# Loading the key weight in two halves, normalising tiles 0 and 3 in halves, and a new order of the whole program

## The chip, the core and the metric

The kernel runs on one core of one Trainium2 chip. The metric is the device time of one execution in microseconds (us), as the median of three runs. A core has five engines that run side by side, each with its own queue that it works through in order: PE (TensorE, the matrix products; the trace lists its weight loads apart as PEld), DVE (VectorE), ACT (ScalarE), POOL (GpSimd) and SP (SyncE, which here only issues DMA transfers). An engine waits at an instruction until what it reads is written, and everything behind it in its queue waits too. The products go to PSUM, which has eight banks; a bank can be written again only when the reader of its last contents is done.

## The reference, cut to what matters

```python
x = A_x                                   # 1 x 2048 x 512, bf16
h = x + _A_ref(_layernorm(x), A_wqkv, A_wo)
h2 = h + _B_ref(_layernorm(h), B_w1, B_w2)

def _A_ref(x, wqkv, wo):                  # linear attention, 32 heads of 16
    q, k, v = split(x @ wqkv)
    phi = lambda t: jnp.where(t > 0, t + 1, jnp.exp(t)) + 1e-6
    pq, pk = phi(q), phi(k)
    kv = jnp.einsum("bhsd,bhse->bhde", pk, v)
    z = jnp.einsum("bhsd->bhd", pk)
    num = jnp.einsum("bhqd,bhde->bhqe", pq, kv)
    den = jnp.einsum("bhqd,bhd->bhq", pq, z)[..., None] + 1e-6
    return (num / den) @ wo

def _B_ref(x, w1, w2):                    # 512 -> 1792 -> 512
    return jnp.maximum(x @ w1, 0) @ w2
```

## The kernel before

The 2048 rows of x are cut into 16 tiles of 128 rows, and four tiles make a chunk. The whole program is one list of words, ORDER. A loop reads it from left to right and calls one small function for each word, and each function puts its instructions at the end of the queues of its engines. So the order of the words is the order of each engine's queue; nothing else schedules. The last lines of the kernel are that loop:

```python
    for word in ORDER.split():
        name, *idx = word.split(".")
        ops[name](*map(int, idx))
```

The words, in the order of the work (t is a tile, c a chunk, b a PSUM bank):

- `lx.t.n` loads n tiles of x, `lk.k.n`, `lq`, `lv`, `lo`, `l1`, `l2` load n of the K-slices of the weights of keys, queries, values, output and of the two dense layers. All are DMA transfers that SP issues.
- `warm.n.b.w` runs n products on zeros, before there is data.
- `S.t` and `A.t` (DVE) take mean and variance of a row; `R.t.n` (ACT, two activations) makes 1/sqrt(var + eps) for n tiles; `N.t` (DVE, line 268) writes the normalised tile to `h_nat`. `N.t.k.n` does so for n column blocks of 128 from block k on.
- For the tiles 0 to 4, `T.t.b` (PE, line 293, four products with the identity) transposes the normalised tile into bank b and `E.t` (ACT, line 303) copies it to `lnT`. `T.t.b.k.n` and `E.t.k.n` do n of the four blocks. The other tiles are transposed by a DMA, `X.t` (line 314).
- `K.t.b` (PE, line 322) is the key product of a tile, four matmuls over the four K-slices; `K.t.b.k.n` does n of them. `F`, `U` (ACT) and `M`, `D` (DVE) make phi of it. `Q.c.j.b`, `qF`, `qU`, `qM`, `qD` do the same for the queries.
- `G.t` (PE, line 374) sums key times normalised x over the tiles; `za`, `zf`, `zhi`, `zlo` (DVE) sum the keys themselves, and `z.j.b` (PE, line 398) finishes z. `kv`, `m`, `d4`, `dl4`, `dx4`, `wb`, `rb`, `ab`, `dm` make the product with values and output weight, and the denominator, which goes through DRAM and comes back spread over the partitions (`rb`, `ab`).
- `h.t.b` (PE, line 502) and `hD.t` (DVE) give h; `s`, `a`, `r`, `n` normalise it, and `x.t` (SP, line 315) transposes it by DMA into `lnT` of its chunk.
- `p.c.f.b` and, in halves of the columns, `ph` (PE, lines 517 and 526) are the first dense layer, `pD.c.f.2` (DVE, line 537) its relu for two of the 14 slices; `f.t.b.f0.n` (PE, line 546) is the second layer, `fo.t` (DVE, line 554) adds h, and `fd.t` writes the result.

The key product takes its pieces by two arguments:

```python
    def op_K(t, b, k=0, n=KD):
        ...
        for kd in range(k, k + n):
            nc.tensor.matmul(
                bk[:, b, :], lhsT=lnT[c][:, kd, j * P : (j + 1) * P], rhs=wk_sb[:, kd, :],
                **part(("k", t), KD),
            )
```

Of the kernel before, what the change touches and what calls it, by code (L numbers as in the profile page):

```python
# [23 lines left out]
R.8.2 G.0 S.15 F.4.2 N.8 G.1 S.13 X.8 U.4.2 S.14 G.3 qU.0.2.2 A.13 S.12 lv.0.2 G.2 M.4.2 A.12 N.9 K.7.3 R.12.2
A.15 D.4.2 X.9 qF.0.2.2 K.6.2 N.12 A.14 S.11 R.14.2 X.12 K.8.0 F.6.2 N.15 N.14 G.4 A.11 N.13 U.6.2 M.6.2 X.13
qM.0.0.2 K.9.1 R.10.2 qD.0.0.2 K.12.2 X.15 D.6.2 U.8.2 za.4.1 G.5 F.8.2 X.14 K.13.3 N.11 N.10 za.6.0 G.6 X.11
U.12.2 G.7 M.8.2 F.12.2 X.10 qM.0.2.2 K.14.0 D.8.2 M.12.2 K.15.1 lv.2.2 za.8.0 l1.0.2 K.11.3 l1.2.2 F.14.2 D.12.2
K.10.2 zf U.14.2 qD.0.2.2 G.9 zhi F.10.2 M.14.2 G.13 zlo U.10.2 G.8 M.10.2 D.14.2 G.12 D.10.2 z.0.0 z.2.0 z.3.0
# [568 lines left out]
```

## Time and profile before

| | |
|---|---|
| time, median of 3 runs | 169.2 us (169.2 to 169.52) |
| the profiled execution's own time | 169.35 us |
| its span, first to last instruction | 167.6 us |
| PE busy, instructions | 162.9 us, 97%, 920 products |
| DVE busy | 115.9 us, 69% |
| ACT busy | 49.5 us, 30% |
| mean granted TensorE clock | 0.999 |
| DMA | 16.28 MB, mean 97 GB/s |

The profile's page gives the busy time of each engine and its share of the span. Between the span and the time of the execution lie 1.75 us that the profile does not show. The chain of waits follows the execution back from its last instruction; each of its rows has a start, a length, and the instructions with their line. A timeline row has the start, the busy time, the engine, the line, the operation, what it writes and reads, and in brackets how long the engine had been idle and who ended that. A row of the windows view has, for one stretch, the length and then the busy time of each engine with its number of instructions.

### The profile page before, as it was taken

How to read it: one execution, taken by the hardware profiler on the slowest of the kernel's cores; microseconds unless marked ns; L12 is line 12 of the kernel's file. 1: busy time of each engine (PE TensorE's matmuls, PEld its weight loads, DVE VectorE, ACT ScalarE, POOL GpSimd, SP SyncE). 2: the span in 40 equal slices, each digit the busy share in tenths (PEclk: the TensorE clock that was granted, in tenths of full speed). 3: DMA queues.
4: the chain of work that ended last, by engine and by line, in shares of the span. 5: the costliest groups of instructions: out<-in, count | busy, mean ns of one | idle time of the engine just before them, and what ended most of it. 6: DMA issues, size and time to landing. Idle time of an engine off the chain costs nothing.

```text
span 167.6 us, 2414 instructions
## 1 busy us (share of the span) xinstructions
PE 162.9 (97%) x920; PEld 79.8 (48%) x920; DVE 115.9 (69%) x215; ACT 49.5 (30%) x83; POOL 4.8 (3%) x21
## 2 busy tenths in 40 slices
PE   7899999999999999999999999999999999999992
PEld 7444444454544674444444444444444444564441
DVE  3899999952499979668999899564535484400632
ACT  3799997625687925300000020010000000000000
POOL 7400000000000000000000000000000000000000
PEclk9999999999999999999999999999999999999999
DMA  4974464773651546140353034312000000020131
GB/s 108 353 294 118 107 121 94 246 288 94 153 195 36 124 126 218 60 133 29 101 98 88 0 61 89 104 30 64 0 0 4 31 0 0 21 83 2 47 104 60
DMA packets 26091, 16.28 MB, mean 97 GB/s; under 512 B 16096, under 2 KB 25056, under 8 KB 26080
## 3 DMA queue, kind: packets, MB, share of 16 engines
q1 hardware_dynamic: 25760, 15.87, 33.5%
q10 hardware_dynamic: 320, 0.26, 0.6%
q8 instruction: 7, 0.11, 0.3%
q14 instruction: 4, 0.03, 0.1%
HBM read 9.96 MB, written 2.62 MB: 75 GB/s over the span
## 4 chain that ended last, share of the span: by engine, by line
PE 93%; DVE 2%; DMA 1%; ACT 1%; issue 0%
PE bk L546 28%; PE bk L517 26%; PE bk L374 8%; PE bk L322 8%; PE bk L330 8%; PE bk L502 8%; PE bk L526 3%; DMA x_nat<-in_A_x_dram 1%; DVE st L254 1%; PE bk L446 1%; DVE gT L554 1%; PE bk L398 1%; DVE h_nat L268 1%; PE bk L420 1%; PE bk L432 1%; PE bk L293 1%
## 5 line engine op out<-in xcount | busy, mean ns | idle before, releaser
L546 PE MATMUL bk<-w_sb,at 128*128 128x512 bf16 (+2 forms) x252 | 50.9, 355 | 0.0
L517 PE MATMUL bk<-lnT,w_sb 128*128 128x512 bf16 x200 | 45.6, 379 | 0.0
L537 DVE TENSOR_SCALAR at<-bk 128x1024 bf16<-128x1024 f32 x27 | 32.4, 1221 | 13.6 <-PE bk L517 10.6
L546 PEld LDWEIGHTS <-at 128*128 128x128 bf16 x252 | 23.5, 98 | 25.2 <-DVE at L537 0.3
L517 PEld LDWEIGHTS <-w_sb 128*128 128x128 bf16 x200 | 19.5, 98 | 23.1 <-issue 0.4
L554 DVE SCALAR_TENSOR_TENSOR gT<-bk,rstd,h_nat 128x512 bf16<-128x512 f32 (+2 forms) x18 | 12.1, 688 | 22.6 <-PE bk L546 20.2
L340 ACT ACTIVATE eb<-bk 128x1024 bf16<-128x1024 f32 (+1 forms) x18 | 16.6, 930 | 3.5 <-PE bk L420 1.6
L260 ACT ACTIVATE rstd<-mv,eps 128x2 f32<-128x2 f32 (+2 forms) x14 | 4.1, 295 | 45.1 <-DVE mv L257 41.6
L343 ACT ACTIVATE rb<-bk 128x1024 bf16<-128x1024 f32 (+1 forms) x18 | 16.6, 935 | 0.9 <-PE bk L322 0.9
L502 PE MATMUL bk<-m_sb,pqs 128*128 128x512 bf16 x64 | 15.3, 379 | 0.0
L322 PE MATMUL bk<-wk_sb,lnT 128*128 128x512 bf16 x64 | 15.0, 379 | 0.0
L330 PE MATMUL bk<-lnT,wq_sb 128*128 128x512 bf16 x64 | 15.0, 379 | 0.0
L374 PE MATMUL bk<-at,h_nat 128*128 128x512 bf16 x56 | 13.2, 379 | 0.0
L254 DVE BATCH_NORM_STATS2 st<-x_nat 128x6 f32<-128x512 bf16 x16 | 10.5, 676 | 2.1 <-DMA x_nat<-in_A_x_dram 2.1
L508 DVE TENSOR_TENSOR h_nat<-bk,x_nat 128x512 bf16<-128x512 f32 x16 | 10.7, 679 | 1.1 <-PE bk L502 1.0
L256 DVE BATCH_NORM_STATS2 st<-h_nat 128x6 f32<-128x512 bf16 x16 | 10.8, 686 | 0.2
L502 PEld LDWEIGHTS <-pqs 128*128 128x128 bf16 x64 | 6.3, 98 | 7.6
L374 PEld LDWEIGHTS <-h_nat 128*128 128x128 bf16 x64 | 6.1, 97 | 7.3 <-issue 0.2
L322 PEld LDWEIGHTS <-lnT 128*128 128x128 bf16 x64 | 6.0, 98 | 7.4 <-DMA lnT<-h_nat 0.4
L330 PEld LDWEIGHTS <-wq_sb 128*128 128x128 bf16 x64 | 6.1, 98 | 7.1 <-issue 0.2
L347 DVE TENSOR_SCALAR eb<-eb 128x1024 bf16<-128x1024 bf16 (+1 forms) x18 | 6.7, 390 | 0.3 <-ACT eb L340 0.3
L268 DVE TENSOR_SCALAR h_nat<-x_nat,mv,rstd 128x512 bf16<-128x512 bf16 x16 | 6.2, 406 | 0.6 <-ACT rstd L261 0.5
(62 smaller groups left out, 90.9 us busy)
## 6 DMA issues: line engine op xcount, KB each, us to landing
w_sb<-in_B_w_dram SPq DMA_DIRECT2D x4, 896.0 KB, 5.2
out_dram<-gT SPq DMA_DIRECT2D x15, 128.0 KB, 1.9
rr<-scr SPq DMA_DIRECT2D x28, 64.0 KB, 2.6
x_nat<-in_A_x_dram SPq DMA_DIRECT2D x2, 512.0 KB, 7.0
x_nat<-in_A_x_dram SPq DMA_DIRECT2D x4, 128.0 KB, 2.7
wk_sb<-in_A_wqkv_dram SPq DMA_DIRECT2D x1, 512.0 KB, 4.1
x_nat<-in_A_x_dram SPq DMA_DIRECT2D x2, 256.0 KB, 4.4
wq_sb<-in_A_wqkv_dram SPq DMA_DIRECT2D x1, 512.0 KB, 5.8
```

The source lines that it names most:

```text
L254: op_S = lambda t: nc.vector.bn_stats(out=st[:, t, :], in_=x_nat[:, t, :])
L256: op_s = lambda t: nc.vector.bn_stats(out=st2[:, t, :], in_=h_nat[:, t, :])
L322: nc.tensor.matmul(bk[:, b, :], lhsT=lnT[c][:, kd, j * P : (j + 1) * P], rhs=wk_sb[:, kd, :], **part(("k", t), KD),)
L330: nc.tensor.matmul(bk[:, b, :], lhsT=wq_sb[:, kd, j * P : (j + 1) * P], rhs=lnT[c][:, kd, :], start=(kd == 0), stop=(kd == KD - 1),)
L340: nc.scalar.activation(out=buf(eb, kind, i, n), in_=bank(at_bank[kind, i], n), func=ACT.Exp)
L343: nc.scalar.activation(out=buf(rb, kind, i, n), in_=bank(at_bank[kind, i], n), func=ACT.Relu)
L374: nc.tensor.matmul(bk[:, KD + kd, :], lhsT=ln_nat[:, t, kd * P : (kd + 1) * P], rhs=pk(t)[:, 0, :], start=(not stated), stop=(len(stated) ...
L502: nc.tensor.matmul(bk[:, b, :], lhsT=pqs[:, (c * KD + jb) % NQ, j * P : (j + 1) * P], rhs=m_sb[:, jb, :], start=(jb == 0), stop=(jb == KD ...
L517: nc.tensor.matmul(bk[:, b, :], lhsT=w1_sb[:, kd, f * P : (f + 1) * P], rhs=lnT[c][:, kd, :], start=(kd == 0), stop=(kd == KD - 1),)
L537: nc.vector.tensor_scalar(out=acts[c % 2][:, f : f + n, :], in0=bank(at_bank["p", c, f], n), scalar1=-1.0, scalar2=0.0, op0=ALU.mult, op1= ...
L546: nc.tensor.matmul(bk[:, b, 0 : w * P], lhsT=acts[c % 2][:, f, j * P : (j + 1) * P], rhs=w2_sb[:, f, k * P : (k + w) * P], **part(("f", t, ...
L554: nc.vector.scalar_tensor_tensor(out=o_t[:, t % NO, cols], in0=bk[:, at_bank["f", t, k], 0 : w * P], scalar=rstd2[:, t : t + 1], in1=h_nat ...
```

## The change

Only the list of words changes. Its line numbers grow by one, since the new list is one line longer.

- The key weight is loaded by two transfers, `lk.0.2` and `lk.2.2`, with tile 3 of x between them, in place of one transfer ahead of tile 3. The query weight now goes ahead of the tiles 6 and 7.
- DVE takes the mean and variance of tile 2 before it normalises any tile; then it normalises tile 1, tile 0 in two halves, and tile 2. Tile 3 is normalised in two halves, with other work between.
- PE transposes tile 1 first, then tile 0 in two halves and tile 2. The first key products are of tiles 1 and 2, each in two halves; those of tile 0 and tile 3 follow, in halves too.
- From there on the list has the same words in another order and with other banks: the loads of the value and output weights, the keys, the sums, the heads, the two dense layers.

```diff
-table const lx.0.1 warm.66.7.64 lx.1.1 masks lx.2.1 lk.0.4 lx.3.1 S.0 lx.4.2 S.1 lx.6.2 lq.0.4 A.0 A.1 S.2 R.0.1
-warm.2.7 lx.8.4 R.1.1 N.0 lx.12.4 A.2 N.1 T.0.1 R.2.1 T.1.6 E.0 N.2 E.1 T.2.4 S.3 K.0.2 E.2 A.3 S.4 K.1.4.2.2
...
+table const lx.0.1 warm.66.7.64 lx.1.1 masks lx.2.1 lk.0.2 lx.3.1 S.0 lk.2.2 S.1 lx.4.2 lq.0.4 A.0 A.1 S.2
+warm.2.7 R.1.1 lx.6.2 R.0.1 lx.8.4 A.2 N.1 R.2.1 lx.12.4 N.0.2.2 T.1.0 N.0.0.2 N.2 T.0.6.0.2 T.0.2.2.2 E.1 S.3
...
```

The loads at the start of SP's queue, before (`x_nat` is x, 512 columns a tile; `wk_sb` and `wq_sb` are the weights of keys and queries, four K-slices of 512):

```order
L220 DMA x_nat<-in_A_x_dram 128x512 x3
L226 DMA wk_sb<-in_A_wqkv_dram 128x4x512
L220 DMA x_nat<-in_A_x_dram 128x512
L220 DMA x_nat<-in_A_x_dram 128x1024 x2
L226 DMA wq_sb<-in_A_wqkv_dram 128x4x512
L220 DMA x_nat<-in_A_x_dram 128x2048 x2
```

and after:

```order
L221 DMA x_nat<-in_A_x_dram 128x512 x3
L227 DMA wk_sb<-in_A_wqkv_dram 128x2x512
L221 DMA x_nat<-in_A_x_dram 128x512
L227 DMA wk_sb<-in_A_wqkv_dram 128x2x512
L221 DMA x_nat<-in_A_x_dram 128x1024
L227 DMA wq_sb<-in_A_wqkv_dram 128x4x512
L221 DMA x_nat<-in_A_x_dram 128x1024
L221 DMA x_nat<-in_A_x_dram 128x2048 x2
```

The first three tiles of x stay where they were; tile 3 moves ahead of the second half of the key weight, and the query weight ahead of the tiles 6 and 7.

The first statistics and normalisations on DVE, before (`st` and `mv` are what `S` and `A` write, `h_nat` what `N` writes):

```order
L254 BN_STATS st<-x_nat 128x6 x2
L255 BN_AGGR mv<-st 128x2 x2
L254 BN_STATS st<-x_nat 128x6
L268 TENSOR_SCALAR h_nat<-x_nat,mv,rstd 128x512
L255 BN_AGGR mv<-st 128x2
L268 TENSOR_SCALAR h_nat<-x_nat,mv,rstd 128x512 x2
L254 BN_STATS st<-x_nat 128x6
L255 BN_AGGR mv<-st 128x2
```

and after:

```order
L255 BN_STATS st<-x_nat 128x6 x2
L256 BN_AGGR mv<-st 128x2 x2
L255 BN_STATS st<-x_nat 128x6
L256 BN_AGGR mv<-st 128x2
L269 TENSOR_SCALAR h_nat<-x_nat,mv,rstd 128x512
L269 TENSOR_SCALAR h_nat<-x_nat,mv,rstd 128x256 x2
L269 TENSOR_SCALAR h_nat<-x_nat,mv,rstd 128x512
L255 BN_STATS st<-x_nat 128x6
L256 BN_AGGR mv<-st 128x2
```

The statistics of tile 2 (the third `BN_STATS` and the `BN_AGGR` behind it) now stand ahead of all normalisations; the first of these is tile 1's, and tile 0's are the two of 256 columns.

The DMA transposes of chunk 3 (`lnT_88`) in SP's queue, with the last one of chunk 2 (`lnT_87`) and the writes of results around them, before:

```order
L315 DMA_TRANSPOSE lnT_87<-hn 128x4x128 x4
L561 DMA out_dram<-gT 128x512
L315 DMA_TRANSPOSE lnT_88<-hn 128x4x128
L561 DMA out_dram<-gT 128x512 x2
L315 DMA_TRANSPOSE lnT_88<-hn 128x4x128 x2
L561 DMA out_dram<-gT 128x512
L315 DMA_TRANSPOSE lnT_88<-hn 128x4x128
```

and after:

```order
L316 DMA_TRANSPOSE lnT_87<-hn 128x4x128 x2
L562 DMA out_dram<-gT 128x512
L316 DMA_TRANSPOSE lnT_87<-hn 128x4x128 x2
L316 DMA_TRANSPOSE lnT_88<-hn 128x4x128 x3
L562 DMA out_dram<-gT 128x512
L316 DMA_TRANSPOSE lnT_88<-hn 128x4x128
```

Before, the last transpose of chunk 2 and the four of chunk 3 had writes between them; after, `x.11`, `x.8`, `x.12`, `x.14` and `x.15` follow each other, then one write and `x.13`. In PE's order three products of chunk 2 (`p.2.6`, `p.2.7`, `p.2.2`) now stand ahead of the first of chunk 3, `p.3.4`; before, eleven of the fourteen stood ahead of `p.3.2`.

More of the change, by code (lines that the diff above doesn't have):

```diff
@@ L24 @@
[L24 to L28, printed above, removed]
@@ new lines @@
+z.3.1 G.9 zc zh d4.0.0 G.10 dl4.0 dx4.0 G.15 wb.0 G.14 Q.1.0.2 gA.2.2 gD.0.2 rb.0.0 Q.1.1.3 ab.0.1 rb.0.6 ab.0.5
+kv.2.7 rb.0.4 kv.0.7 ab.0.7 kv.3.7 rb.0.2 kv.1.7 qF.1.0.2 Q.1.2.0 l2.7.7 kx ab.0.3 Q.1.3.1 qM.1.0.2 qU.1.0.2 m.3.7
+m.0.4 m.1.5 qU.1.2.2 qD.1.0.2 m.2.6 Q.2.0.2 mD.0.2 mA.2.2 Q.2.1.3 qF.1.2.2 dm.0.0.2 Q.2.3.7 dm.0.2.2 qF.2.0.2
+h.1.1 qM.1.2.2 qD.1.2.2 qU.2.0.2 h.0.4 hD.1 Q.2.2.6 s.1 d4.1.0 a.1 hD.0 nA.1 h.3.2 s.0 qF.2.2.2 x.1 h.2.1 a.0 hD.3
+nA.0 Q.3.3.3 s.3 qU.2.2.2 x.0 hD.2 Q.3.2.2 dl4.1 a.3 n.3 Q.3.1.5 s.2 qF.3.2.2 x.3 Q.3.0.4 a.2 n.2 qU.3.2.2
@@ new lines @@
+qM.3.2.2 x.2 qM.2.0.2 ph.0.11.1.0 qM.2.2.2 dx4.1 ph.0.1.7.0 qD.3.2.2 qU.3.0.2 ph.0.0.6.0 wb.1 ph.0.2.2.0 l2.0.7
+ph.0.10.0.0 qF.3.0.2 ph.0.3.3.0 ph.0.10.0.1 qM.3.0.2 rb.1.2 ph.0.0.6.1 qD.2.0.2 rb.1.7 ph.0.11.1.1 rb.1.3 p.0.5.5
+pD.0.10.2 rb.1.1 p.0.4.4 rb.1.5 qD.3.0.2 rb.1.0 p.0.7.1 rb.1.6 pA.0.4.2 qD.2.2.2 ph.0.1.7.1 d4.2.4.2 pD.0.0.2
+ph.0.2.2.1 dl4.2 rb.1.4 ph.0.3.3.1 dl4.3 p.0.6.0 pD.0.2.2 dx4.2 p.0.12.6 dx4.3 wb.2 r.0.4 p.0.13.7 dm.1.2.2
+p.0.8.4 dm.1.0.2 pD.0.12.2 p.0.9.5 rb.2.6 rb.2.4 h.7.2 rb.2.1 wb.3 h.6.7 rb.2.2 hD.7 rb.2.0 pD.0.6.2 h.4.6 rb.2.3
@@ new lines @@
+rb.2.7 f.0.3.0.7 rb.2.5 pD.0.8.2 hD.4 f.0.3.7.7 s.7 a.7 hD.6 h.5.6 s.4 f.3.1.7.7 n.7 dm.2.2.2 s.6 f.3.1.0.7
+dm.2.0.2 hD.5 rb.3.2 h.10.2 rb.3.5 a.4 s.5 rb.3.7 fo.3 h.8.6 rb.3.4 rb.3.1 a.5 hD.10 h.11.7 rb.3.6 a.6 n.5 rb.3.0
+n.4 f.2.1.0.7 n.6 rb.3.3 s.10 x.5 hD.8 f.2.1.7.7 hD.11 x.7 fo.0 s.8 h.9.5 fd.3 dm.3.2.2 x.6 f.1.0.0.7 dm.3.0.2
+fo.2 x.4 hD.9 h.12.4 s.9 h.15.6 a.10 h.13.3 h.14.5 hD.13 hD.12 f.1.0.7.7 hD.15 hD.14 p.1.6.2 s.12 s.11 p.1.12.4
+s.15 p.1.5.7 s.13 p.1.7.3 a.11 fo.1 n.11 p.1.10.5 pD.1.6.2 p.1.11.6 a.12 a.13 a.8 s.14 p.1.9.1 a.9 a.15 n.10 r.8.4
@@ new lines @@
+p.1.8.0 pD.1.10.2 x.10 p.1.3.3 pD.1.8.2 p.1.13.5 a.14 n.12 r.12.4 p.1.1.1 n.14 n.9 r.4.4 pD.1.12.2 x.9 p.1.0.0
+p.1.2.2 pD.1.0.2 fd.0 x.11 p.1.4.6 n.13 pD.1.2.2 f.6.4.7.7 pD.1.4.2 f.6.4.0.7 n.15 n.8 x.8 f.5.7.0.7 x.12
+f.7.0.0.7 x.14 f.4.5.0.7 x.15 f.4.5.7.7 fd.2 x.13 p.2.6.2 fd.1 p.2.7.3 p.2.2.1 pD.2.6.2 p.3.4.6 fo.4 p.2.3.2
+f.7.0.7.7 pD.2.2.2 fo.6 f.5.7.7.7 fo.7 fd.6 fd.7 p.2.12.4 fo.5 p.2.13.5 p.3.3.2 pD.2.12.2 p.3.2.1 p.2.10.0
+pD.3.2.2 p.3.8.4 p.2.11.1 p.2.4.3 pD.2.10.2 p.3.5.7 p.3.0.1 pD.3.4.2 p.3.9.5 p.3.7.6 pD.3.8.2 p.3.1.2 p.2.5.4
@@ L54 @@
+pD.3.0.2 p.3.6.5 pD.2.4.2 p.2.0.2 pD.3.6.2 p.2.9.7 p.2.1.3 p.3.13.5 p.3.12.4 p.2.8.6 p.3.10.0 pD.2.8.2 p.3.11.1
+f.13.7.0.7 pD.3.10.2 pD.2.0.2 f.10.6.7.7 pD.3.12.2 f.8.1.7.7 f.8.1.0.7 f.15.3.0.14.0.2 f.15.5.0.14.3.1 f.10.6.0.7
+fo.15.3.1 fd.15.3.1 fd.4 f.14.2.7.7 fo.8 f.14.2.0.7 fo.10 fd.8 fd.5 fo.15.0.2 f.13.7.7.7 fd.10 fd.15.0.2
+f.11.1.0.7 f.11.1.7.7 f.9.6.7.7 fo.11 fo.13 f.9.6.0.7 fd.13 fd.11 f.12.0.0.7 fo.9 fo.14 fd.9 f.12.0.7.7 fd.14
+f.15.5.0.14.2.1 fo.12 fo.15.2.1 fd.12 fd.15.2.1
 """
```

37 lines of the change are left out of this document (9 added, 28 removed).

## The prediction

> **What bounds the kernel now.** I read the page first, then the windows, then the chain of waits, and last the timeline of the first microseconds. The page has PE at 97%; the windows tell where the other 3% lie.
>
> ```profile
> 6.02:7.12 1.10, 1.04 (x8) 0.74 (x8) 0.80 (x4) 0.94 (x3) 0.16 (x1) 1.00 1.05 375
> ...
> 8.30:40.00 31.70, 31.70 (x191) 14.66 (x190) 27.19 (x69) 24.36 (x42) 0.00 (x0) 1.00 0.58 169
> 40.00:104.00 64.00, 64.00 (x340) 31.33 (x339) 55.41 (x99) 20.30 (x29) 0.00 (x0) 1.00 0.39 104
> 104.00:163.70 59.70, 59.70 (x298) 28.26 (x298) 27.26 (x30) 0.50 (x2) 0.00 (x0) 1.00 0.13 37
> ```
>
> From 8.30 to 163.70 PE is busy in every microsecond; what it lacks of 100% lies ahead and behind. So the end comes from three things alone: when PE gets its first real products, whether it ever waits after that, and the 3.9 us from 163.70 to the end of the span. The chain of waits says the same and gives the pace.
>
> ```profile
> 7.12 0.40 PE bk L293 x4
> 7.52 1.80 PE bk L322 x8
> 9.32 0.24 PE bk L293 x4
> 9.57 1.73 PE bk L322 x8
> ...
> 94.46 8.63 PE bk L517 x40
> ...
> 163.71 0.77 DVE gT L554
> ```
>
> Forty products of 512 columns take 8.63, so one takes 0.216 and four (one word `K`, `Q`, `h` or `p`) 0.863. The first eight key products take 1.80 where the next eight take 1.73: here PE waits about 0.08, on bank 4, which `E.2` must empty before `K.1` may write it. What set the start is in the timeline:
>
> ```profile
> 3.04 1.29 DVE L254 BATCH_NORM_STATS2 st<-x_nat 128x6 f32<-128x512 bf16 x2 [1.80 <-DMA x_nat<-in_A_x_dram]
> 4.24 0.30 DVE L255 BATCH_NORM_AGGREGATE mv<-st 128x2 f32<-128x6 f32 x2
> 4.84 0.69 DVE L254 BATCH_NORM_STATS2 st<-x_nat 128x6 f32<-128x512 bf16 x1 [0.30 <-DMA x_nat<-in_A_x_dram]
> 5.46 0.52 DVE L268 TENSOR_SCALAR h_nat<-x_nat,mv,rstd 128x512 bf16<-128x512 bf16 x1
> 5.89 0.16 DVE L255 BATCH_NORM_AGGREGATE mv<-st 128x2 f32<-128x6 f32 x1
> 5.98 0.38 DVE L268 TENSOR_SCALAR h_nat<-x_nat,mv,rstd 128x512 bf16<-128x512 bf16 x1
> 6.66 0.41 DVE L268 TENSOR_SCALAR h_nat<-x_nat,mv,rstd 128x512 bf16<-128x512 bf16 x1 [0.30 <-ACT rstd L261]
> ...
> 6.03 1.49 PE L293 MATMUL bk<-ident,h_nat 128*128 128x128 bf16 x12 [0.43 <-DVE h_nat L268]
> ...
> 6.67 1.09 ACT L303 ACTIVATE lnT<-bk 128x512 bf16<-128x512 bf16 x2
> ...
> 7.36 0.59 PE L322 MATMUL bk<-wk_sb,lnT 128*128 128x512 bf16 x2
> ```
>
> `S.2` waits for tile 2 of x until 4.84 and ends at 5.53; `N.0` ends at 5.98, `T.0` starts at 6.03, `E.0` at 6.67, and the first key product at 7.36, behind `T.2`, which waited for `N.2`.
>
> **The change part by part.** *The loads.* The weight is not what is waited for:
>
> ```profile
> wk_sb<-in_A_wqkv_dram SPq DMA_DIRECT2D x1, 512.0 KB, 4.1
> ...
> wq_sb<-in_A_wqkv_dram SPq DMA_DIRECT2D x1, 512.0 KB, 5.8
> ...
> 2.18 0.43 SPq L226 DMA_DIRECT2D wk_sb<-in_A_wqkv_dram  x1
> ...
> 4.16 0.43 SPq L226 DMA_DIRECT2D wq_sb<-in_A_wqkv_dram  x1
> ```
>
> Issued at 2.18 it lands at 6.3, 1.1 before the first key product. In two halves one more issue of 0.43 goes through SP, which waits for nothing there; the second half ends behind tile 3's 128 KB, a quarter of the 512 KB more, and is used two products (0.43) after the first. Gain nothing, cost nothing: the cover is those 1.1 us, and half a microsecond of lateness would cost nothing either. The tiles 0 to 2 of x are issued as before, so `S.2` keeps its 4.84 to 5.53. The query weight moves ahead of tiles 6 and 7, so these land where it does now, at 4.16 plus 5.8, 10.0. Their statistics stand on DVE behind `D.1`, and ahead of that lie the first key product (to 8.3), its exp, its relu, and a sum, some half a microsecond each, so nothing waits long for them.
>
> *The new chain to the first key product.* `A` ends 0.21 behind the last `S` (4.33 to 4.54), so `A.2` ends at 5.74; `N.1` behind an `A` took until 6.36, 0.31 after 6.05, so now until 6.05; its transposes start 0.05 later, 6.10; `E` followed `T` by 0.64, so `E.1` starts at 6.74 and, at 0.60, ends at 7.34; the key product followed the end of `E.0` (7.27) by 0.09, so `K.1` starts at 7.43. `N.2` no longer waits for its `rstd`, and `T.2` is through at about 7.2: no longer last. Before, `K.0` started at 7.36 and PE lost 0.08 behind it, in effect 7.44. Now nothing is lost there, since `K.2` finds its copy ready at 8.2, before its turn at 8.29. **The start is worth 0.01, that is nothing**: `T.2` was relieved, and `E.1` is late in its place.
>
> *The halves on DVE.* No row has 256 columns; the nearest are
>
> ```profile
> L347 DVE TENSOR_SCALAR eb<-eb 128x1024 bf16<-128x1024 bf16 x14 | 5.6, 420 | 0.3 <-ACT eb L340 0.3
> L347 DVE TENSOR_SCALAR eb<-eb 128x512 bf16<-128x512 bf16 x4 | 1.1, 284 | 0.0
> ```
>
> Twice 284 is 148 ns more than 420, so an instruction's fixed part is at most 0.15 and the two added ones cost 0 to 0.30. I take 0.2, since back-to-back instructions overlap (5.89 plus 0.16, and the next starts at 5.98). The Trainium skill (VectorE: DVE Perf Modes, section on the TRN2 errata) says that every SBUF operation pays a fixed latency and that tiles should keep at least 512 elements, which speaks against these halves; it measures the fixed part as about 150 cycles of 0.96 GHz, an estimate of 0.31 for two. The rows agree with it, and by it the sum would take the upper end.
>
> Does PE see the 0.2? DVE is full in two stretches:
>
> ```profile
> 20.00:35.00 15.00, 15.00 (x71) 6.75 (x70) 14.94 (x32) 11.91 (x17) 0.00 (x0) 1.00 0.67 180
> 86.00:106.00 20.00, 20.00 (x95) 9.02 (x93) 18.93 (x36) 0.90 (x4) 0.00 (x0) 1.00 0.31 67
> ```
>
> ```profile
> 8.70 0.41 DVE L268 TENSOR_SCALAR h_nat<-x_nat,mv,rstd 128x512 bf16<-128x512 bf16 x1 [0.24 <-ACT rstd L261]
> ...
> 34.05 1.29 DVE L350 TENSOR_TENSOR at<-rb,eb 128x1024 bf16<-128x1024 bf16 x2
> ...
> 35.56 0.19 PE L398 MATMUL bk<-ones,zhl 128*128 128x1 bf16 x2
> ```
>
> In the first it hands over the last keys at 35.34 and the z products start at 35.56, a slack of 0.2; besides, DVE stood idle 0.24 for `R.3` ahead of `N.3`, where the new order has `S.5`. Nothing, then, with that idle time as its cover; the slack of 0.2 stays.
>
> *The rest of the order.* PE has the same products, so its work is the same. What can cost is a place where it arrives early. I went through the new queues with the durations above. Two places have nothing to spare. `K.4` comes one query product behind `T.4`: PE's way is 0.24 plus 0.86, and the way over the copy 0.40 (row 7.12) plus 0.60 plus 0.09, both about 1.1. And `K.3` is due 12 products and four transposes behind 7.43, at 10.26, and needs the first half of `E.3`.
>
> ```profile
> 9.60 0.60 ACT L303 ACTIVATE lnT<-bk 128x512 bf16<-128x512 bf16 x1
> ```
>
> `E.3` ended at 10.20; now half of `E.0` stands ahead of it and half of itself behind, so its first half ends at 10.2 again, and with 0.09 to PE that is 10.29. Each place may cost 0 to 0.1; I take 0.1 for both. A copy, a transpose or a relu that comes earlier than needed costs nothing, and the other handovers keep some tenths by the same counting. The end of the list is the same: one `fo`, one quarter `fo`, two writes.
>
> The sum: 169.35 − 0.01 + 0 + 0.1 = 169.45 for the profiled execution, which stands 0.15 over the median; against the median **169.3 us**.
>
> **The rivals.** *DVE is late at z* (slower). If a half costs as much as a whole, 0.41 (row at 6.66), DVE has 0.8 more to do ahead of the z products, less the 0.2 of slack: 0.6 later, 169.9. It decides from 0.2 on. For it: DVE is at 14.94 of 15 there. Against it: the 0.24 of idle time recovered, and the L347 rows. Chance 0.14.
>
> *`x.13` is late* (slower). Chunk 3 starts earlier on PE:
>
> ```profile
> 91.00 2.59 PE bk L517 x12
> ...
> 96.59 0.85 DVE L276 TENSOR_SCALAR hn<-h_nat,mv 128x512 bf16<-128x512 bf16 x3
> ...
> 99.82 2.35 DVE L537 TENSOR_SCALAR at<-bk 128x1024 bf16<-128x1024 f32 x2
> ...
> 20.29 9.22 SPq L314 DMA_TRANSPOSE lnT<-h_nat  x7
> ...
> 97.46 4.95 SPq L315 DMA_TRANSPOSE lnT<-hn  x3
> ...
> DMA to landing us min/median/max: 2.4/2.5/4.3
> ```
>
> Chunk 1's products start at 91.00 plus one `h` word, 91.86; the fourteen end at 103.9, six `f` words of seven products at 113.0, three products of chunk 2 at 115.6: there `p.3.4` is due. DVE gets its first four products at 95.3 and has seven relus of 1.14 (2.35 for two, with an overlap), 8.0, and seven `n` of 0.26 and 1.1 of statistics, 2.9, ahead of the end of `n.8`: 106.2. Then `x.8`, `x.12`, `x.14`, `x.15` at 1.3 (9.22 for seven), a write's issue of 0.4 (as the weight's), and `x.13`, which lands 2.5 later: 114.3. It has 1.3 to spare. But three in a row took 4.95 once, 1.0 more than at 1.3 each, and one landed after 4.3: with one of these PE waits 0 to 0.6, with both 1.6. I price it at 0.6: 169.9. Chance 0.08.
>
> *Other handovers are missed*: the 0.1 to 0.4 of slack is worked out from one execution, over many places. Missing by 0.4 more in one gives 169.7. Chance 0.16.
>
> *Tile 2 of x lands early* (faster).
>
> ```profile
> x_nat<-in_A_x_dram SPq DMA_DIRECT2D x4, 128.0 KB, 2.7
> ```
>
> Tile 2 is issued just ahead of the weight's 2.18, so at 1.7, and lands at 4.8; by the median of its kind, 2.7, it would land at 4.4. Then `S.2` would start behind `A.1` at 4.5, and all that follows be 0.3 to 0.4 earlier: 168.85. For it: a smaller transfer stands behind it. Against it: nothing ahead of it changes. Chance 0.16.
>
> *The first transposes run fast* (no measurable change). Eight took 1.04 from 6.02 on, so four 0.5, and four take 0.24 at 9.32: PE is slow until about 7. At the fast pace `E.1` and with it `K.1` start some 0.2 earlier, and `T.2`, through at 7.2, allows it: 169.1. Before, this would have gained nothing, since `T.2` waited for `N.2`. The Trainium skill (TensorE: Matmul & The Clock Gate, part 1) has the clock released at the end of a free-running window of activity, so at another time in another execution; no row here shows it move. Chance 0.10.
>
> **How the numbers follow.** What a measurement here can tell from no change is about 0.2%, 0.34 us: 168.86 to 169.54. The forecast, 169.3, has 0.36, and with the fast transposes the same verdict has 0.46; their own range is 169.0 to 169.5. Late at z 0.14, `x.13` 0.08 and other handovers 0.16 make slower 0.38. Faster is the early tile, 0.16. The range takes in the early tile with the fast transposes, 168.85 − 0.2, and the slower rivals, 169.9, with the upper end of the halves, 0.1 more: 168.65 to 170.0; outside lie two of the late handovers together, and a start earlier still, less than 0.2.
>
> **What would show it.** Right: `K.1` first, at 7.4 to 7.5, PE full from there to about 163.8, and the key products without the 1.80. Wrong: a PE wait after 7.5. In the chain of waits it would stand as DVE between `G` and z near 35, as a DMA of `lnT` near 115, or as ACT `lnT` near 10 or 14. A first key product before 7.1 would make the start worth more than I say.

## The result and the profile after

The changed kernel takes 170.13 us in the median of ten runs (168.87 to 170.45), the kernel before 169.2 in ten runs beside them (168.79 to 169.55): 1.005 times as long, with a 95% interval of 1.0035 to 1.0066. I had forecast 169.3, no measurable change, and a range up to 170.0. The profiled execution took 169.87, its span is 168.2.

The windows of the changed kernel, in the columns known from before:

```profile
5.66:6.96 1.30, 1.27 (x12) 0.94 (x13) 1.30 (x4) 0.85 (x3) 0.42 (x2) 1.00 0.65 165
6.96:16.00 9.04, 8.63 (x46) 3.67 (x45) 7.69 (x24) 8.23 (x21) 0.00 (x0) 1.00 0.68 237
16.00:40.00 24.00, 24.00 (x150) 11.08 (x149) 20.32 (x49) 17.45 (x26) 0.00 (x0) 1.00 0.65 174
40.00:104.00 64.00, 64.00 (x341) 31.38 (x339) 53.99 (x98) 20.78 (x31) 0.00 (x0) 1.00 0.38 93
104.00:164.20 60.20, 60.20 (x301) 28.50 (x299) 27.51 (x31) 0.00 (x0) 0.00 (x0) 1.00 0.16 43
```

From 16.00 on PE is full, as before. Nearly all that was lost lies in the first 16 us. The timeline of PE there:

```profile
5.67 1.40 PE L294 MATMUL bk<-ident,h_nat 128*128 128x128 bf16 x12
6.96 0.60 PE L323 MATMUL bk<-wk_sb,lnT 128*128 128x512 bf16 x2
7.72 1.45 PE L323 MATMUL bk<-wk_sb,lnT 128*128 128x512 bf16 x6 [0.16 <-DMA wk_sb<-in_A_wqkv_dram]
9.39 0.29 PE L294 MATMUL bk<-ident,h_nat 128*128 128x128 bf16 x2 [0.21 <-DVE h_nat L269]
...
13.28 0.40 PE L294 MATMUL bk<-ident,h_nat 128*128 128x128 bf16 x4
13.52 1.03 PE L331 MATMUL bk<-lnT,wq_sb 128*128 128x512 bf16 x4
14.42 1.04 PE L323 MATMUL bk<-wk_sb,lnT 128*128 128x512 bf16 x4
```

The first key product starts at 6.96, 0.40 ahead of the 7.36 of before. Then PE waits three times: in the middle of `K.1`, for the second half of the weight, at `T.3` and at `T.4`. The brackets show less than is lost, since the end of a matmul is modelled; from start to start, less the pace of 0.216 of a product, the three cost 0.32, 0.38 and 0.20, and two handovers (`K.4`, and `K.11` at 30.9) 0.04 each: 0.98. Before, 0.08 and 0.03 were lost so. Together: −0.40 + 0.98 − 0.11 = +0.47; the last product starts 0.50 later (164.74, was 164.24). The two profiled executions lie 0.52 apart (169.87 and 169.35) and the medians 0.93, so this account covers the profiled pair and not all of the difference of the medians.

What DVE did meanwhile:

```profile
4.41 0.66 DVE L255 BATCH_NORM_STATS2 st<-x_nat 128x6 f32<-128x512 bf16 x1
...
7.19 0.18 DVE L256 BATCH_NORM_AGGREGATE mv<-st 128x2 f32<-128x6 f32 x1
8.39 0.69 DVE L255 BATCH_NORM_STATS2 st<-x_nat 128x6 f32<-128x512 bf16 x1 [1.02 <-DMA x_nat<-in_A_x_dram]
9.00 0.33 DVE L269 TENSOR_SCALAR h_nat<-x_nat,mv,rstd 128x256 bf16<-128x256 bf16 x1
...
11.23 1.29 DVE L255 BATCH_NORM_STATS2 st<-x_nat 128x6 f32<-128x512 bf16 x2 [0.19 <-DMA x_nat<-in_A_x_dram]
12.44 0.40 DVE L269 TENSOR_SCALAR h_nat<-x_nat,mv,rstd 128x512 bf16<-128x512 bf16 x1
12.75 0.17 DVE L256 BATCH_NORM_AGGREGATE mv<-st 128x2 f32<-128x6 f32 x1
12.84 0.38 DVE L269 TENSOR_SCALAR h_nat<-x_nat,mv,rstd 128x512 bf16<-128x512 bf16 x1
```

`S.2` no longer waits for tile 2. But `S.5` stands still for 1.02 until tiles 4 and 5 are there, with the first half of `N.3` behind it (9.00), and `T.3` behind that; `S.7` waits for tiles 6 and 7 until 11.23, and `N.4`, for `T.4`, comes two statistics later, at 12.84. The issue rows of the changed kernel (size of one, median time to landing) show that the loads came later:

```profile
x_nat<-in_A_x_dram SPq DMA_DIRECT2D x4, 128.0 KB, 2.3
wk_sb<-in_A_wqkv_dram SPq DMA_DIRECT2D x2, 256.0 KB, 3.8
x_nat<-in_A_x_dram SPq DMA_DIRECT2D x2, 256.0 KB, 5.6
```

The 3.8 is the middle of two unlike halves, and the 5.6 (4.4 before) that of two pairs of tiles. By the completion records of the trace, in which each transfer reports in sixteen parts, the weight's first half is complete at 5.25, 3.1 after its issue, and its second half at 7.68, 4.5 after its issue; the whole one was complete at 6.32, 4.1 after. Of the second half's sixteen parts fourteen had landed by 6.65; two came at 7.15 and 7.68, and PE waits for the last. Of the whole weight's parts the first landed at 5.79 and the last at 6.32. Tiles 4 and 5 are complete at 8.37 (before, 7.31), and tiles 6 and 7, which now stand behind the query weight as well, at 11.21 (8.46). All landing times below are read so, by the last part.

### The profile page after: what moved, and what is told of

The parts are those of the page before. It is cut to its first block, busy times and chain, and to the rows that moved or that the text cites. A ratio compares the mean times of both kernels' runs of the same rounds, so it can differ in the third digit from the quotient of the medians.

```text
span 168.2 us, 2408 instructions
## 1 busy us (share of the span) xinstructions
PE 163.4 (97%) x920; PEld 79.8 (47%) x920; DVE 114.9 (68%) x217; ACT 49.7 (30%) x85; POOL 4.7 (3%) x21
## 4 chain that ended last, share of the span: by engine, by line
PE 93%; DVE 2%; ACT 2%; DMA 1%; issue 0%
PE bk L547 29%; PE bk L518 26%; PE bk L375 8%; PE bk L503 8%; PE bk L331 8%; PE bk L323 7%; PE bk L527 3%; DMA x_nat<-in_A_x_dram 1%; DVE st L255 1%; ACT lnT L304 1%; PE bk L294 1%; PE bk L447 1%; PE bk L399 1%; PE bk L421 1%; PE bk L433 1%; DVE h_nat L269 0%
## 5 line engine op out<-in xcount | busy, mean ns | idle before, releaser
L547 PE MATMUL bk<-w_sb,at 128*128 128x512 bf16 (+2 forms) x252 | 49.7, 355 | 0.0
L518 PE MATMUL bk<-lnT,w_sb 128*128 128x512 bf16 x200 | 44.0, 379 | 0.0
L323 PE MATMUL bk<-wk_sb,lnT 128*128 128x512 bf16 x64 | 15.5, 379 | 0.2 <-DMA wk_sb<-in_A_wqkv_dram 0.2
L269 DVE TENSOR_SCALAR h_nat<-x_nat,mv,rstd 128x512 bf16<-128x512 bf16 (+1 forms) x18 | 6.7, 393 | 0.0
```

The lines of the kernel that those rows point to most:

```text
L323: nc.tensor.matmul(bk[:, b, :], lhsT=lnT[c][:, kd, j * P : (j + 1) * P], rhs=wk_sb[:, kd, :], **part(("k", t), KD),)
L518: nc.tensor.matmul(bk[:, b, :], lhsT=w1_sb[:, kd, f * P : (f + 1) * P], rhs=lnT[c][:, kd, :], start=(kd == 0), stop=(kd == KD - 1),)
L547: nc.tensor.matmul(bk[:, b, 0 : w * P], lhsT=acts[c % 2][:, f, j * P : (j + 1) * P], rhs=w2_sb[:, f, k * P : (k + w) * P], **part(("f", t, ...
```

## The experiments

Nearly all edit only words of ORDER; split_cols and late_issue add a small load function. The table gives the median, the ratio to the kernel before on the same chip with its interval, the share of time in which the transfer engines were busy from 5.50 to 7.50 (windows of that kernel's profile), and the landings there of the last of the weight, of tiles 4 and 5 and of tiles 6 and 7. The share adds up the times of all packets, so it can pass 1. Share and landings are those of one execution, the time is a median.

| kernel | us | ratio (95%) | share | weight | 4, 5 | 6, 7 |
|---|---|---|---|---|---|---|
| before | 169.2 | | 1.12 | 6.32 | 7.31 | 8.46 |
| before_again | 169.26, one run | | 1.09 | 6.71 | 7.74 | 9.07 |
| changed | 170.13 | 1.005 (1.0035 to 1.0066) | 0.71 | 7.68 | 8.37 | 11.21 |
| s5_late | 170.06 | 1.006 (1.0041 to 1.0078) | 0.78 | 7.41 | 8.12 | 11.28 |
| n4_early | 170.6 | 1.009 (1.0067 to 1.0112) | 0.75 | 7.12 | 8.40 | 11.24 |
| s5_n4 | 169.91 | 1.0069 (1.0034 to 1.0104) | 0.69 | 7.46 | 8.79 | 11.22 |
| split_before | 169.65 | 1.0037 (1.0022 to 1.0052) | 0.68 | 7.74 | 9.46 | 10.17 |
| whole | 169.25 | 1.0001 (0.9984 to 1.0018) | 0.99 | 6.57 | 7.60 | 9.93 |
| whole_x67 | 168.95 | 1.0 (0.9983 to 1.0017) | 1.06 | 6.41 | 7.43 | 8.16 |
| whole_x67_s5 | 169.72 | 1.0036 (1.0023 to 1.0049) | 1.07 | 6.19 | 7.21 | 8.68 |
| x3_first | 168.95 | 0.9996 (0.9981 to 1.0011) | 1.07 | 6.62 | 7.29 | 7.98 |
| adjacent | 169.79 | 1.0043 (1.0021 to 1.0066) | 0.95 | 5.84 | 7.10 | 8.04 |
| split_cols | 169.89 | 1.0042 (1.0026 to 1.0057) | 0.74 | 6.23 | 8.38 | 9.03 |
| split_touch | 169.78 | 1.0039 (1.0023 to 1.0056) | 0.82 | 7.67 | 8.71 | 9.38 |
| four_pieces | 169.86 | 1.004 (1.002 to 1.0061) | 0.94 | 6.11 | 8.63 | 9.28 |
| more_tiles | 169.04 | 0.9994 (0.9979 to 1.001) | 1.07 | 6.05 | 7.45 | 8.15 |
| wq_split | 168.92 | 0.999 (0.9972 to 1.0007) | 1.07 | 6.35 | 7.38 | 8.05 |
| other_queue | 170.82 | 1.0084 (1.0048 to 1.0119) | 1.01 | 7.00 | 8.01 | 8.73 |
| late_issue | 170.04 | 1.0072 (1.0049 to 1.0095) | 0.77 | 7.04 | 8.49 | 9.68 |
| split_lead | 169.22 | 1.0031 (1.0006 to 1.0055) | 0.78 | 7.75 | 8.41 | 9.53 |

### Is it the order of DVE?

Theory 1 took the three waits as a series in which the last decides. First, the statistics out of the way of `N.3`:

```diff
- R.3.1 S.5 K.2.3.0.2 ... N.3.0.2 A.5 S.4 T.3.5.0.2 ... N.3.2.2 E.3.0.2
+ R.3.1 K.2.3.0.2 ... N.3.0.2 T.3.5.0.2 ... N.3.2.2 S.5 A.5 S.4 E.3.0.2
```

> The changed kernel with one edit: S.5 A.5 S.4 stand behind both halves of N.3 on DVE, no longer ahead of them. In the changed kernel DVE stood idle 1.02 us at S.5 for the tiles 4 and 5 of x (8.37), and PE waited 0.38 us for the first half of N.3 behind it (transposes at 9.39). Theory 1, the waits stand in series and the last one, N.4 for T.4 at 13.28, sets PE's place whatever came before it: T.3 starts 0.35 to 0.4 earlier, at 9.0, but T.4 still starts at 13.2 to 13.3, behind S.7 that waits for tiles 6 and 7 until 11.2; the time stays 170.1 (169.95 to 170.25). Rival, every wait counts by itself: 170.13 - 0.38 = 169.75.

`T.3` starts at 8.83, and nothing is won. The timeline of s5_late shows where the time went:

```profile
10.67 1.04 PE L331 MATMUL bk<-lnT,wq_sb 128*128 128x512 bf16 x4 [0.16 <-DMA wq_sb<-in_A_wqkv_dram]
...
13.35 0.40 PE L294 MATMUL bk<-ident,h_nat 128*128 128x128 bf16 x4 [0.34 <-DVE h_nat L269]
```

PE arrives early at the query product, waits for its weight, then at `T.4`, which starts at 13.35 instead of 13.28. Then `N.4` out of the way of tiles 6 and 7, alone and with the first edit:

```diff
- E.3.2.2 S.7 Q.0.0.6 ... F.0.1 S.6 K.3.5.2.2 U.0.1 N.5 Q.0.2.0 A.7 N.4 F.3.1
+ E.3.2.2 Q.0.0.6 ... F.0.1 N.4 K.3.5.2.2 U.0.1 N.5 Q.0.2.0 S.7 S.6 A.7 F.3.1
```

> The changed kernel with one edit: N.4 and N.5 stand ahead of S.7 and S.6 on DVE, so they no longer wait for tiles 6 and 7 of x (11.21). N.4 then starts when its rstd is there, 11.5, and T.4 may start at 12.0, 0.6 ahead of its turn. Theory 1 (waits in series) and the rival (each counts) agree here: the 0.20 us that PE waited at T.4 go, 170.13 - 0.20 = 169.93. If the 0.20 do not go, T.4 waits for something else than N.4, and neither holds: 170.1.

> The changed kernel with both edits of DVE's order: S.5 A.5 S.4 behind the halves of N.3, and N.4, N.5 ahead of S.7 and S.6. Theory 1: now T.4 is free to come as early as PE is there, so both waits go: 170.13 - 0.38 - 0.20 = 169.55, and only the 0.32 us at the second half of K.1, for the second half of the weight, is left. If the first edit alone changed nothing and the second alone 0.2, this is 0.6 against either sum of 0.2: that is what tells waits in series. Rival: the sum of the two single gains, whatever they are; and if the tiles of x land 1 us late whatever the order, 169.9 or more.

Both sums missed: 170.6 for 169.93, and 169.91 for 169.55. ACT of n4_early:

```profile
13.74 0.29 ACT L261 ACTIVATE rstd<-mv,eps 128x2 f32<-128x2 f32 x1 [0.69 <-DVE mv L256]
14.07 0.20 ACT L262 ACTIVATE rstd<-rstd 128x2 f32<-128x2 f32 x1
14.18 0.58 ACT L304 ACTIVATE lnT<-bk 128x512 bf16<-128x512 bf16 x1
```

`R.6` waits here for the statistics of tiles 6 and 7, and `E.4`, which `K.4` needs, stands behind it; besides, `N.4` now holds `S.7` up until its own rstd comes (11.56). I had left ACT's queue out. So the series has one link more, and behind it stands the landing at 11.2: `K.4` starts at 14.42 in the changed kernel, 14.49, 14.81 and 14.39 in these three. None of these orders of DVE frees it. In the two with `N.4` early, `S.7` starts behind `N.5`, at 12.21 and 11.79, and so later than the landing; a better order is not excluded.

### Is it the loads?

The change's load in the kernel before, and the loads of before in the changed kernel, in two steps:

```diff
 split_before, an edit of before:
- lk.0.4 lx.3.1 S.0 lx.4.2
+ lk.0.2 lx.3.1 S.0 lk.2.2 lx.4.2
 whole, an edit of the changed kernel:
- lk.0.2 lx.3.1 S.0 lk.2.2 S.1
+ lk.0.4 lx.3.1 S.0 S.1
 whole_x67, besides:
- lq.0.4 A.0 ... R.1.1 lx.6.2 R.0.1
+ lx.6.2 A.0 ... R.1.1 lq.0.4 R.0.1
```

> The kernel before with one edit: the key weight in two halves with tile 3 of x between them, all else in its old order. Theory 2, the split makes the weight's second half and all loads behind it land late (7.7 where the whole weight landed at 6.3; tiles 4 and 5 at 8.4 where it was 7.3): K.0 starts at 7.75 instead of 7.36, and N.3 stands behind S.4, which waits for tiles 4 and 5: 169.2 + 0.4 = 169.6 (to 169.8 with a wait at T.3). Rival, the late landing belongs to the executions shown and not to the split: 169.2, with the second half landing at 6.6. In both, if tile 2 of x lands near 4.2 again and not at 4.8, its early landing in the changed kernel comes from the smaller transfer behind it.

> The changed kernel with one edit: the key weight in one piece again (ahead of tile 3 of x), all else as changed, so the query weight still stands ahead of tiles 6 and 7. Theory 2 (the split itself starves the loads): the pause of the transfers between 5.5 and 7.5 goes, the whole weight lands near 6.3 and tiles 4 and 5 near 7.4 instead of 8.1 to 8.8; K.1 has no wait in its middle and T.3 none (0.32 and 0.38 go); tiles 6 and 7 land at 10.0 to 10.4 instead of 11.2, so T.4 starts near 12.4 and PE is 0.7 to 0.9 us ahead of the changed kernel: 169.3 to 169.4. Rival, the moved query weight alone makes tiles 6 and 7 late: they land at 11 as before the edit, T.4 at 13.2, 170.1. If tile 2 lands near 4.8 instead of near 4.0, the early tile came from the smaller piece, and 0.4 of the gain is given back in the first transposes, but not at T.4.

> The changed kernel with the loads in the order of the kernel before: key weight in one piece, tiles 6 and 7 of x ahead of the query weight. Orders of PE, DVE and ACT as changed. Theory 2: tiles 6 and 7 land near 8.5 and the query weight near 10.0, all before their turns; no wait of PE is left behind the first key product but the handovers of some hundredths: if tile 2 lands near 4.0, the first key product starts near 7.0 and the time is 168.7 to 168.9, faster than before; if it lands near 4.8, 169.1. Rival, the new order of DVE and ACT is late by itself (halves, S.5, N.4): waits at T.3 and T.4 stay and the time is 169.5 or more.

The cut alone makes the kernel before 0.6 slower (169.65 beside 169.05), and undone alone it brings the changed kernel from 170.13 to 169.25, at a ratio of 1.0001. In whole the waits inside `K.1` and at `T.4` are gone; 0.38 is left at `T.3`, which I had expected to go too. PE of split_before waits at the same two places, for the second half and, behind tiles 4 and 5, at `T.3` (its profiled run is its slowest of twelve, 170.72, so these waits are more than the median shows):

```profile
7.79 1.46 PE L322 MATMUL bk<-wk_sb,lnT 128*128 128x512 bf16 x6 [0.41 <-DMA wk_sb<-in_A_wqkv_dram]
10.55 0.40 PE L293 MATMUL bk<-ident,h_nat 128*128 128x128 bf16 x4 [1.31 <-DVE h_nat L268]
```

The place of the query weight moves the median by 0.3 at most (169.25 to 168.95), which the two ratios do not separate. whole_x67 is the whole change but for the loads; 168.95 is just over the 168.7 to 168.9 expected, and the time of before (169.0). Its PE:

```profile
6.77 1.89 PE L323 MATMUL bk<-wk_sb,lnT 128*128 128x512 bf16 x8
8.70 0.28 PE L294 MATMUL bk<-ident,h_nat 128*128 128x128 bf16 x2
...
12.44 0.39 PE L294 MATMUL bk<-ident,h_nat 128*128 128x128 bf16 x4
...
13.53 1.03 PE L323 MATMUL bk<-wk_sb,lnT 128*128 128x512 bf16 x4
```

No wait inside the first key products, none at `T.4`; 0.21 is left at `T.3`. Two tries at that rest, s5_late's edit on whole_x67, and tile 3 ahead of the whole weight (`lx.3.1 lk.0.4`):

> The changed kernel with the loads in the order of the kernel before, and S.5 A.5 S.4 behind both halves of N.3 on DVE. With those loads alone PE still waited 0.21 at T.3, for the first half of N.3 behind S.5 (tiles 4 and 5 landed at 7.43). Theory 1 with 2: N.3 starts when its rstd is there, 8.15, and T.3 waits for nothing from 8.5 on; that is the last wait near the start, so it counts: 168.95 - 0.2 = 168.75, 0.25 faster than the 169.0 of before. Rival, T.4 or K.4 takes the wait over as it did with the split weight: 168.95.

> The changed kernel's orders of PE, DVE and ACT with whole loads: tiles 0 to 3 of x, the key weight in one piece, tiles 4 to 7, the query weight. With tile 3 behind the weight PE waited 0.21 at T.3: S.3 started when tile 3 landed, 6.79, and N.3 stood behind it. Here tile 3 lands near 4.3 and S.3 starts when DVE is free, 6.5; the weight lands 0.35 later, 6.5 to 6.9, still ahead of the first key product near 7.0. Expected 168.75, 0.3 faster than before. Rival, the weight comes too late in most runs (over 7.0): 169.0 to 169.2.

The first is 0.6 slower than before (169.72 beside 169.09). Its DVE stands idle where `S.5` stood, and is that much later at `N.4`, so that `T.4` starts at 13.00:

```profile
8.12 0.60 DVE L269 TENSOR_SCALAR h_nat<-x_nat,mv,rstd 128x256 bf16<-128x256 bf16 x2 [0.65 <-ACT rstd L262]
```

With loads on time the changed order had `S.5` in the right place. In x3_first `T.3` no longer waits (8.60), and the median is 168.95, which its ratio of 0.9996 does not tell from before; two of its twelve executions took 171.47 and 171.78, at a mean granted clock of 0.99. So none of these versions beats both kernels measurably.

### What in the cut?

Theory 2a and 2c blame rows of the weight that were not read before, 2b the number of transfers, 2d each start of a weight transfer. All are edits of before: the halves without tile 3 between (`lk.0.2 lk.2.2 lx.3.1`); split_before with a tiny transfer by ACT ahead of everything; halves by columns (`wk_sb[:, :, 0:256]`, then the rest); tiles 4 and 5 apart (`lx.4.1 ... lx.5.1`).

> The kernel before with the key weight in two halves, one right behind the other, tile 3 of x behind both. Theory 2a, the second half brings rows of the weight that nothing has touched yet, and the first reading of such rows stalls the transfers (in the one-piece load all rows are touched at its start, where transfers were also slow, 3.1 to 4.4): a pause from about 5 on, tiles 4 and 5 near 8 to 8.4, time 169.5 to 169.7 as with tile 3 between. Theory 2b, the tile between is what costs: no pause, second half at 6.3, tiles 4 and 5 at 7.3, time as before, 169.05 to 169.2.

> The kernel before with the split load (halves with tile 3 between), plus one tiny transfer at the very start, issued by ACT: eight bytes of each of eight rows of the weight, one in every 64 rows, into an unused tile. Theory 2a (first reading of far rows stalls): with the rows' neighbourhoods touched ahead, the pause at 5.5 to 7.5 goes or shrinks, second half near 6.3, tiles 4 and 5 near 7.4, time 169.0 to 169.2. Rival 2b (more transfers in the queue, whatever their addresses): the pause stays, 169.65.

> The kernel before with the key weight in two transfers again, one right behind the other, but cut by columns: each brings 256 columns of all 512 rows, so that the second reads on rows that the first has read. Theory 2c (first reading of far rows): no pause near 5 to 7, 169.0 to 169.2 (its packets are half as long, and for that it may lose some tenths of landing time that the weight has to spare). Theory 2b (one transfer more) or one by which any cut of the weight costs: 169.6 to 169.8, as with the cut by rows.

> The kernel before with the key weight whole and one transfer more all the same: tiles 4 and 5 of x in two transfers. Theory 2b, the number of transfers in the queue makes the pause near 6: 169.5 to 169.7, as with the split weight. Theory 2c, it is the weight's second half, as a transfer that begins on rows not read before, that makes it: no pause, 169.0 (one issue of 0.45 more ahead of the query weight costs nothing there).

Every cut of the key weight costs about the same, 0.6 to 0.8, by rows or by columns, with eight rows touched or not; one more transfer of x costs nothing. (The profiled run of adjacent is its fastest of ten, 168.69; its share, 0.95, shows hardly a pause.) Addresses fall with split_cols, the mere number with more_tiles. Then four pieces (`lk.0.1 lk.1.1 lk.2.1 lk.3.1`), the query weight in two (`lq.0.2 lq.2.2`), and the second half on ACT's queue:

> The kernel before with the key weight in four transfers of 128 KB, one right behind the other, tile 3 of x behind them. Theory 2d, every start of a weight transfer while others are under way stalls the engines for some tenths: three more starts instead of one, tiles 4 and 5 land at 9 or later, time 170.2 to 171.5. Rival 2e, the engines pause once, behind the first short weight transfer, however many follow (what matters is that no long transfer is queued): 169.6 to 169.8 as with two.

> The kernel before with the key weight whole and the query weight in two transfers (two K-slices each), one right behind the other. Theory 2d (every start of a weight transfer): a pause behind the second half's start, near 8.5 to 10, the loads of tiles 8 to 15 land about 1 us later than 11.5 and 13; the time may stay at 169.0, since those have more slack. Rival 2e (only what stands early, when nothing long is queued): no pause, tiles 8 to 11 near 11.5, time 169.0.

> The kernel before with the key weight's second half issued by ACT, right behind its table load near 2.1, so on another queue; the first half and everything else on SP's queue as before. If the pause hangs on the order within one queue (a short weight transfer and then another behind it), it goes: whole weight by 6.4, tiles 4 and 5 near 7.4, 169.0 to 169.2. If two weight transfers cost wherever they stand, tiles 4 and 5 land at 8 or later: 169.6. Tile 2 of x may land some tenths later in both, since the two queues share the engines.

Four pieces are no worse than two, so 2d falls; the query weight, later in the queue, can be cut for nothing. other_queue's time, 170.82, tells little about the loads. ACT's transfer is issued at 0.82 and not at 2.1 as I had assumed and goes ahead of tiles 1 and 2, so that tile 2 lands at 4.64 and PE stands idle 1.46 ahead of `T.0`. Then, from 7.53 to 10.93, the granted clock was 0.50, and the first eight key products took 0.427 each for 0.216: that is 1.7 of the profiled run's 171.11. Three of its seven executions, from 171.11 to 171.77, have a mean granted clock of 0.987 to 0.990. Its landings do tell something: the weight is cut there as well, and the share is 1.01.

What the bad cases share is when their transfers are issued. SP issues one in some 0.47. A transfer of 512 KB keeps the engines for some 1.5 (in the kernel before, the query weight landed 1.46 behind the tiles ahead of it), and SP runs ahead meanwhile: with the weight whole, tiles 4 and 5 were issued 3.1 to 3.3 before the transfer ahead of them was complete (the median of its parts), and took 0.65 to 0.68 from there. In other_queue, with the weight cut but half of it issued at 0.82, it was 3.6, and they took 0.68. Behind the other cut weights the same interval was 1.6 to 2.8, and they took 0.7 to 2.1 (the 0.7 are split_cols, at 2.8, and adjacent, at 2.4: no pause at this place); in three profiles it was 2.9 to 3.2, but there the second half itself had been late, 1.26 to 1.55 where it took 0.72 to 0.89 elsewhere. So theory 4, that this interval, the lead, is what counts: take the lead away with the weight whole, by two tiny transfers of SP behind it, or give some back with it cut, by loading tiles 1 and 2 in one:

```diff
 late_issue, an edit of before (each ts reads eight bytes of 16 rows):
- lk.0.4 lx.3.1
+ lk.0.4 ts.0 ts.1 lx.3.1
 split_lead, an edit of split_before:
- lx.1.1 masks lx.2.1 lk.0.2
+ lx.1.2 masks lk.0.2
```

> The kernel before, key weight whole, with two tiny transfers (eight bytes of each of 16 rows, into an unused tile) issued by SP right behind the weight, so that tile 3, tiles 4 and 5, tiles 6 and 7 and the query weight are issued some 0.95 later: 2.2 to 2.6 ahead of their turn instead of 3.1 to 3.5. Theory 4 (what counts is how far ahead of its turn a transfer is issued): tiles 4 and 5 pause as behind a cut weight, 1.0 to 2.1 from tile 3's median landing to theirs, and land at 7.7 or later; 169.5 to 170. Rival (it is the cut of the weight itself): 0.68, tiles 4 and 5 at 7.3 to 7.5, time 169.1.

> The kernel before with the key weight cut as in the change (halves with tile 3 between) and tiles 1 and 2 of x in one transfer, so that everything behind them is issued 0.47 earlier: 2.6 to 2.9 ahead of its turn instead of 2.2 to 2.4. Theory 4: the pause shrinks, tiles 4 and 5 take 0.7 to 0.9 behind the weight's second half instead of 1.05 to 2.1, and land near 7.2. Rival (the cut itself): 1.05 to 2.1 as before, landing at 8. Its time says little, since tile 1 lands later and S.1 and S.2 with it: the start is some 0.4 later, 169.4 to 170 either way.

The rows of 5.50 to 7.50, share and GB/s last: the changed kernel,

```profile
5.50:7.50 2.00, 1.92 (x15) 1.15 (x15) 1.84 (x6) 1.55 (x5) 0.58 (x2) 1.00 0.71 199
```

more_tiles,

```profile
5.50:7.50 2.00, 1.69 (x16) 0.99 (x17) 1.68 (x5) 1.97 (x6) 0.67 (x3) 1.00 1.07 367
```

and late_issue:

```profile
5.50:7.50 2.00, 1.53 (x15) 0.84 (x15) 0.69 (x2) 1.97 (x5) 0.67 (x3) 1.00 0.77 258
```

With the weight whole and the issues later, a pause is there too: the share falls from 1.07 to 0.77, tiles 4 and 5 land at 8.49, and the time is 170.04, 1.1 over before. So the cut itself is not needed for it. But the late issue is not isolated by this run. Tiles 4 and 5 took 0.83 behind tile 3, between the 1.0 of theory 4 and the 0.68 of its rival. The weight itself, issued at 2.19 as before, was complete only at 7.04, later than in the eight profiles with nothing put behind it (6.05 to 6.71). And the tiny transfers stand in the queue too; no run issues late without them. split_lead settles nothing: its ratio, 1.0031, is not to be told from split_before's 1.0037, and in its profiled run the pause is whole, tiles 4 and 5 taking 1.60 where I had expected 0.7 to 0.9. Nor is the lead a sharp bound: in the changed kernel tile 3 alone ran at full pace (0.35) with a lead of 2.4. What is shown is that cutting the key weight costs 0.6 to 0.9 through late loads, and that a pause can come without a cut. That the late issue makes it is the reading that fits most rows, and it is not shown; what the engines wait for in the pause is open, and so is why one transfer of 128 KB escapes it.

The last run asked about the base of my sum:

> The kernel before, unchanged, for a second profile of its start. In its first profile tile 2 of x landed at 4.82; in the eight profiles of other kernels since then it landed between 3.9 and 4.6. Theory 3, the late tile belonged to that execution (169.35, where the median of its runs is 169.0): here it lands near 4.0, the first key product starts near 7.0, and the span is 167.1 to 167.4. Rival, the whole weight and six tiles behind it hold tile 2 up in this kernel: 4.8 again.

Tile 2 landed at 3.93. DVE of before_again:

```profile
4.44 0.66 DVE L254 BATCH_NORM_STATS2 st<-x_nat 128x6 f32<-128x512 bf16 x1
...
7.08 0.69 DVE L254 BATCH_NORM_STATS2 st<-x_nat 128x6 f32<-128x512 bf16 x1 [0.56 <-DMA x_nat<-in_A_x_dram]
```

`S.2` waits for nothing, and `K.0` starts at 6.81; but tile 3 is late (7.06), `S.3` waits, and PE loses 0.46 at `T.3`. So the span is 167.6 all the same, not the 167.1 to 167.4 I had expected.

## Why the prediction was wrong

**The loads** are the step that failed. I wrote "Gain nothing, cost nothing: the cover is those 1.1 us", so the cut of the key weight stood in the sum at 0. The runs have it at 0.6 in the kernel before (169.65 beside 169.05) and at 0.9 in the changed one (170.13, and 169.25 with the weight whole). I placed the second half "behind tile 3's 128 KB", that is by bytes. By bytes it would have landed near 6.6, where tile 3 did before. That holds for fourteen of its sixteen parts; the last landed at 7.68, 0.3 after PE wanted it. I counted the bytes ahead of a transfer, as if the engines were busy throughout; their share of 5.50 to 7.50 was 0.71, where it had been 1.12. Why they pause stays open. The trace of before had a warning: at the 375 GB/s of 6.02 to 7.12 the weight's 512 KB take 1.4, and its row says 4.1 from issue to landing, so most of that landing was not its own bytes. The Trainium skill (DMA: Bandwidth & Descriptors, Rules for kernel authors) says to put many small transfers together into a large one, and calls those under 64 KB mostly overhead. The runs agree with its direction, 169.25 whole for 170.13 cut, but the pieces here are four times that size, and more_tiles and wq_split cut other loads for nothing.

**"Nothing waits long for them"** I wrote of tiles 6 and 7, which I had landing at 10.0. They landed at 11.21 (in whole, at the same place in the queue, at 9.93), and PE lost 0.20 at `T.4`. I had followed `S.6` and `S.7` behind `D.1`, but not on to `N.4`, nor to `R.6` and `E.4`. `S.5` ahead of `N.3` I had put into idle time of DVE; it waited for tiles 4 and 5, and PE lost 0.38 at `T.3`. Late tiles came out there: the rival *other handovers* in kind, at about twice its price of 0.4 with the weight's own wait.

**The start.** The rival *tile 2 lands early* came true, `K.1` at 6.96 for my 7.43, but not by the change: tile 2 landed early in before_again as well. The 4.82 belonged to one execution. With the weight whole the first key product starts at 6.77 in the new order (whole_x67), at 6.81 and 6.76 in the old (before_again and more_tiles); "The start is worth 0.01" holds between them.

**The rest** held. The halves on DVE measure

```profile
L269 DVE TENSOR_SCALAR h_nat<-x_nat,mv,rstd 128x512 bf16<-128x512 bf16 x14 | 5.5, 401 | 0.0
L269 DVE TENSOR_SCALAR h_nat<-x_nat,mv,rstd 128x256 bf16<-128x256 bf16 x4 | 1.4, 364 | 0.0
```

in the changed kernel's groups by shape: twice 364 is 0.33 more than 401, 0.65 of busy time for the two. From start to start, since neighbours overlap, it is less: 0.62 for the halves of `N.0` and 0.49 for those of `N.3`, where a whole one takes 0.33, so some 0.46 in all. I took 0.2 with a bound of 0.30 from 1024 and 512 columns. The Trainium skill's fixed part (VectorE: DVE Perf Modes, section on the TRN2 errata), an estimate of 0.31 for two, is nearer but low as well. PE does not see it: neither z nor `x.13` is waited for, and the rivals at these places fall. `x.13`'s margin was 0.7, not 1.3: it landed at 115.3, used at 115.9. `K.4` lost 0.04, `K.3` nothing. `T.1` and `T.0` ran slow in this execution (0.107 from one product to the next), so that rival did not come in it; in whole_x67 they ran at 0.056. whole_x67, which is this rest, gives 168.95 beside 169.0, the forecast's no change. (The terms of the sum add up to 169.44, not 169.45, which leaves the 169.3.)

## What to carry to other kernels

Before a load is cut in pieces to bring its first part earlier, look at how far ahead of their turn the transfers behind it are issued: here the long transfer let the issuing queue get ahead, the pieces took that lead from everything behind, and the loads behind came late. That the lost lead made them late is likely and not shown, so measure the landings of both versions. Where a wait is moved out of one queue, follow its data through every queue to the next product; here the same late tiles came out at DVE, then at ACT. And take the base of a sum from more than one execution: a landing that is late in one profile (tile 2, at 4.82 and in the next profile at 3.93) can look like the bound of the kernel.
